# Cosformer attention into a squared-ReLU MLP: loading the first half of w_in in four pieces

## The chip, the cores and the metric

The kernel runs on one core of a Trainium2 chip. The metric is the device time of one execution in microseconds, as the median of several executions; lower is better.

## The reference, cut to what matters

Eight batches of eight heads, 576 positions and a head width of 64 go through a linear attention; its output, 4608 tokens of width 512, goes through an MLP of inner width 2048.

```python
def phi(x, c, s):
    r = np.maximum(x, 0.0)
    return np.concatenate([r * c, r * s], axis=-1)
q_p, k_p = phi(q, cos_w, sin_w), phi(k, cos_w, sin_w)
kv = np.einsum('bhsf,bhsd->bhfd', k_p, v)
z = np.sum(k_p, axis=2)
num = np.einsum('bhsf,bhfd->bhsd', q_p, kv)
den = np.einsum('bhsf,bhf->bhs', q_p, z)[..., None] + 1e-06
x = (num / den).transpose(0, 2, 1, 3).reshape(B * S, H * D)
r = np.maximum(x @ w_in, 0.0)          # w_in: 512 x 2048
return (r * r) @ w_out                 # w_out: 2048 x 512
```

All inputs and the output are float32. The kernel multiplies in bf16: the loads of w_in and w_out, which GpSimd (POOL) issues, convert on the way.

## The kernel before, in words

**Tiling.** A batch's 576 positions are four blocks of 128 (j = 0 to 3) and a tail of 64 (j = 4). Two blocks make a "half" of 256 tokens. For one batch the attention makes features of k and q (lines 404 to 410), sums k against v with a column of ones (kz), copies that sum to SBUF (kvz), transposes the q features, multiplies (num), divides (div) and transposes the result into xT, which has the 512 inputs of the MLP as four row blocks (kb) of 128. A row block holds two heads, so kb 0 and 1 come from the first four heads (group g = 0) and kb 2 and 3 from the last four (g = 1).

**The first MLP product.** `declare_plain` (line 712) makes one *pair*: two blocks of 128 inner columns (hb and hb + 1) for one half of tokens. It is eight matmuls of 256 token columns on TensorE (PE), into one PSUM bank. A ReLU on ScalarE (ACT, line 416) empties the bank into `rt`, and a square on VectorE (DVE, line 419) writes `gT`. Batch 0 has eight pairs for each of its two halves. Only the first two pairs, hb = 0 and hb = 2 of half 0, are made in two steps of 128 tokens (`split`), so that the first can begin before the second block's xT is there. From batch 3 on the products use seven multiplications in place of eight, with sums of w_in's blocks (`w1s`) that DVE makes early. The second product (`declare_rows` for batch 0, then `declare_pair`) reads `gT` and w_out (`w2sb`).

**The start.** `prologue` (line 1069) issues the loads of batch 0 on SyncE's queue (SP): k, k's tail, q for j = 0 and 1, v's tail, v in two groups of heads, q for j = 2 and 3, and at the end q's tail, `qt`, in two DMAs. POOL waits until v's tail has landed (line 1090) and then issues w_in in four quarters of 512 columns (`load_w1`, lines 371 to 376). TensorE runs `fill` matmuls on zeros meanwhile. POOL then issues, in the planner's order, the loads of batch 1, w_out in four quarters, and the loads of batch 2. Later batches are loaded from SP.

**What sets the order.** Each engine works through its own list in order, so an instruction that waits holds up all behind it on its engine. The lists are written by a planner (lines 52 to 230) while the program is built. Each operation is declared with its possible engines, a cost, and what it reads and writes. The planner walks forward in a planned time: each engine takes the operation that can begin first, among equals the one with the earliest due time, and the engine, if there is a choice, is settled that way too. PE operations have a slot in place of a due time. `SHIFTS` (lines 21 to 34) changes the due time or slot of single operations by their number, and fixes the engine of some (`23:9.5:ACT`). Data loaded in the prologue enter the plan as `given`, with a time of arrival (lines 1098 to 1106). PSUM has six banks in the pool "F" for all such products. Key ("w1", n) stands for a quarter n of w_in: a pair hb reads ("w1", hb // 4).

Of the kernel before, what the change touches and what calls it, by code (L numbers as in the profile page):

```python
# [18 lines left out]


SHIFTS = """
23:9.5:ACT 37:-0.5 38:1.0 44:17.5:ACT 46:-1.0 53:-0.5 62:11.5 79:-2.0 85:-2.5 89:3.0 93:11.0
108:5.5 144:9.0 152:-2.0 157:9.5:ACT 191:-5.0 194:-1.0 202:-1.5 203:-3.5:ACT 204:2.0 210:3.0
238:2.5 241:2.5 243:5.0 249:-6.0 257:-4.0 260:-2.0 261:-6.0 270:2.5 271:3.5 287:-5.0 325:-2.0
335:-0.5 340:1.5 348:8.5 354:-7.0 364:-19.0 383:1.0 390:-3.5 392:1.0 417:-4.5 487:-5.0 492:1.5
516:-7.5 517:-5.5 530:39.0 533:25.5 546:9.0 563:5.5 565:12.5 573:-8.5 575:5.0 588:13.0 593:4.5
598:-2.0 611:-4.5 617:-5.5 636:-1.5 670:7.5 677:-2.0 690:1.0 698:0.0:DVE 702:22.5 703:-19.5
704:3.5:ACT 706:-4.0 715:2.0 731:-2.5 748:5.0 781:-4.5 783:-6.0 785:-7.0 787:-2.0 790:-1.0
794:-1.5 797:1.0 799:1.0 807:11.0 813:-5.5 817:-4.0 820:-7.0 822:-5.5 836:-3.5 850:-3.5
859:-34.0 860:-15.0 870:1.0 872:-4.0 884:12.0 890:49.0 893:17.0 906:5.5 907:23.5 911:3.0 917:3.0  # L30
936:-3.0 951:-12.5 957:-1.0 958:-1.5 963:-3.5 985:7.0 990:-4.0 998:3.5 1005:-4.5 1009:5.5
1023:-10.0 1024:-8.5 1030:-10.0 1041:-26.0:ACT 1042:-10.5 1133:-13.0 1143:1.5 1155:4.0 1157:3.0
1176:-4.5 1191:4.5 1209:5.5 1247:2.5 1306:-0.5
"""


# [197 lines left out]
def kernel(  # L234
# [9 lines left out]
    nc = tc.nc  # L244
    P = nc.NUM_PARTITIONS
# [4 lines left out]
    KB = DM // P  # L250
# [7 lines left out]
    HBH, KB2, DM2, TP = HB // 2, KB // 2, DM // 2, 2 * P  # L258
# [104 lines left out]
    def load_tail(src, nm, i, b, eng):  # L363
        tail = mem[nm + "t"][:, i]
        for g in range(2):
            eng.dma_start(  # L366
                out=tail[g * TAIL : (g + 1) * TAIL, :, :],
                in_=src[b, g * HH : (g + 1) * HH, MAIN:S, :].rearrange("h p d -> p h d"),
            )

    def load_w1(i, n):
        f0, f1 = i * DFF // n, (i + 1) * DFF // n
        nc.gpsimd.dma_start(  # L373
            out=w1sb[:, :, f0:f1],
            in_=moe_w_in[:, f0:f1].rearrange("(kb p) f -> p kb f", p=P),
        )
# [60 lines left out]
    T_MM, T_MM128, T_MM65, T_TR = 0.1092, 0.0586, 0.0296, 0.066  # L437
    plan = Planner(POOLS, 4.5, ("gs1", "gs2", "gs3", "gs4"), 1.0, SHIFTS)
    add = plan.add
    PROD1, PROD2 = 4 * T_MM, 8 * T_MM  # L440
# [5 lines left out]
    T1, T2, t = {}, {}, 16.4  # L446
    for b in range(B):
        T1[b], T2[b] = t, t + g1_len[b] + att_len / 2
        t = T2[b] + g2_len[b] + att_len / 2
# [51 lines left out]
    def xT_of(b, half):  # L501
        return cached(xTb, (b, half), "xT")
# [196 lines left out]

    def w1_at(kb, hb):
        return w1sb[:, kb, hb * P : (hb + 1) * P]

    def gkey(hb, half):
        return ("g", hb // 2, half)

    def xT_keys(b, half, cs):
        xT = xT_of(b, half)
        return [(xT, c) + g for c in cs for g in (((0,), (1,)) if (b, half) == (0, 0) else ((),))]  # L710

    def declare_plain(b, hb, half, pos, split=False):

        bk, rt = plan.buf("F"), plan.buf("rt")
        xT = xT_of(b, half)
        for c in range(2) if split else (None,):

            def plain(_, c=c):
                c0, c1 = (0, TP) if c is None else (c * P, (c + 1) * P)
                for i in range(2):  # L720
                    for kb in range(KB):
                        mm(
                            bank(bk)[:, i * TP + c0 : i * TP + c1],
                            w1_at(kb, hb + i),
                            at(xT)[:, kb, c0:c1],
                            i == 0 and kb == 0 and c0 == 0,
                            kb == KB - 1,
                        )

            add(  # L730
                ("PE", 8 * (T_MM128 if split else T_MM)), plain,
                r=xT_keys(b, half, (0, 1) if c is None else (c,)) + [("w1", hb // 4)],
                w=[bk], pos=pos + (c or 0) * PROD2,
            )
        add(
            ("ACT", 0.5), lambda _: relu(at(rt), bank(bk).rearrange("p (i c) -> p i c", i=2)), r=[bk], w=[rt],
        )
        add(
            ("DVE", 0.34),
            lambda _: square(gT[:, hb : hb + 2, half * TP : (half + 1) * TP], at(rt)),  # L740
            r=[rt], w=[gkey(hb, half)],
        )
# [3 lines left out]
    def declare_tails(b, hb, pos):  # L746

        bk, rt = plan.buf("F"), plan.buf("rt")
        xT = xTt_of(b)
        gt = cached(gttb, b // 4, "gTt")  # L750

        def tails(_):
            for i in range(2):
                for kb in range(KB):
                    mm(
                        bank(bk)[:, i * TP : (i + 1) * TP].rearrange("p (m c) -> p m c", m=4),
                        w1_at(kb, hb + i),
                        at(xT)[:, :, kb % 2, kb // 2, :],
                        i == 0 and kb == 0,
                        kb == KB - 1,  # L760
                    )

        add(("PE", PROD2), tails, r=[(xT, m) for m in range(4)] + [("w1", hb // 4)], w=[bk], pos=pos)
        add(("ACT", 0.5), lambda _: relu(at(rt), bank(bk).rearrange("p (i c) -> p i c", i=2)), r=[bk], w=[rt])
        add(
            ("DVE", 0.34),
            lambda _: square(at(gt)[:, hb : hb + 2, :], at(rt)),
            r=[rt], w=[(gt, hb // 2)],
        )
# [8 lines left out]
    def declare_w1_sums():  # L778
        for r in range(4):
            a = lambda i, kk, r=r: w1_cols(i, kk, r)  # L780
            s = lambda n, r=r: w1_sum(n, r)
            key = lambda i: ("w1", (i * HBH + 2 * r) // 4)
            for n, in0, in1, op, reads in (
                (1, a(1, 0), a(1, 1), ALU.add, [key(1)]),
                (2, s(1), a(0, 0), ALU.subtract, [key(0), ("w1s", 1, r)]),
                (4, a(0, 1), s(2), ALU.subtract, [key(0), ("w1s", 2, r)]),
                (3, a(0, 0), a(1, 0), ALU.subtract, [key(0), key(1)]),
            ):
                add(
                    ("DVE", 0.34), lambda _, n=n, x=in0, y=in1, op=op, s=s: sub(s(n), x, y, op),  # L790
                    r=reads, w=[("w1s", n, r)],
                )
# [17 lines left out]
    def declare_seven1(b, r, t):  # L810
# [12 lines left out]
        def product(name, off, acc, w, x, first, reads):  # L823
# [11 lines left out]
            seven.__name__ = name  # L835
            add(("PE", PROD1), seven, r=reads, w=[acc], pos=t + off * PROD1)

        key = lambda i: ("w1", (i * HBH + 2 * r) // 4)
        product("P1", 0, A, lambda: w1_cols(0, 0, r), lambda: X(0, 0), True, [key(0), turn] + xk[0])
        add(("ACT", 0.5), lambda _: nc.scalar.copy(out=bank(Bk), in_=bank(A)), r=[A], w=[Bk])  # L840
        product("P2", 5, A, lambda: w1_cols(0, 1, r), lambda: X(1, 0), False, [key(0)] + xk[0])
# [10 lines left out]
            r=[E, u3], w=[(rows[1], 1)],  # L852
# [4 lines left out]
            r=[E, u2], w=[(rows[0], 1)],  # L857
# [210 lines left out]

    def prologue():
        for src, nm, part in (  # L1070
            (k, "k", 0), (k, "kt", 0), (q, "q", 0), (v, "vt", 0), (v, "v", 0), (v, "v", 1), (q, "q", 1), (q, "qt", 0)
        ):
            if nm[1:]:
                load_tail(src, nm[0], 0, 0, nc.sync)
            elif nm == "k":
                load_main(src, nm, 0, 0, nc.sync)
            elif nm == "q":
                load_main(src, nm, 0, 0, nc.sync, [slice(part * J // 2, (part + 1) * J // 2)])
            else:
                h = slice(part * HH, (part + 1) * HH)  # L1080
                nc.sync.dma_start(
                    out=mem["v"][:, 0, h],
                    in_=v[0, h, 0:MAIN, :].rearrange("h (p j) d -> p h j d", j=J),
                )
        nc.vector.memset(zeros, 0.0)
        for t in ("vx", "vxt"):
            nc.vector.memset(mem[t][:, :, :, D:E1], 1.0)
        constants()
        fill(28)
        nc.gpsimd.tensor_copy(out=w1sb[0:1, 0, 0:1], in_=mem["vt"][0:1, 0, 0, 0:1])  # L1090
        for i in range(4):
            load_w1(i, 4)

    def fill(n):
        for _ in range(n):
# [3 lines left out]
    L = lambda nm: loaded[nm, 0]  # L1099
    for keys, t in (  # L1100
        ([L("k")], 6.25), ([L("kt")], 6.7), ([(L("q"), 0)], 8.2), ([L("vt")], 9.0), ([(L("v"), 0)], 10.75),
        ([(L("v"), 1)], 12.15), ([(L("q"), 1)], 14.2), ([L("qt")], 14.6),
    ):
        given(keys, t, lat=0.0)
    for i in range(4):
        given([("w1", i)], 11.7 + 0.01 * i, size=2.6)

    def declare_first():
        feature = lambda nm, j, c: declare_feature(nm, 0, j, c, BOTH)
# [139 lines left out]
        declare_xT_pe(0, j, t + 4.0, BOTH)  # L1249
    for s in range(8):  # L1250
        for i in range(2):
            declare_plain(0, s % 4 * 4 + 2 * i, s // 4, T1[0] + s * 2 * PROD2 + i * PROD2, s == 0)
    declare_load(1, "q", "POOL", 17.0)
    declare_w2_load(0, 19.0, 10.0)
    declare_load(1, "k", "POOL", 20.0)
# [44 lines left out]
        for i, pair in enumerate(PAIRS[b]):  # L1300
            declare_pair(b, pair, T2[b] + i * 7 * PROD2)

    t0 = {"PE": 8.0, "ACT": 6.3, "DVE": 6.3, "SP": 10.0, "POOL": 12.9, "GIVEN": 0.0}
    with tc.manual_schedule():
        prologue()
        end = None
# [35 lines left out]
```

## Time and profile before

| what | value |
|---|---|
| time, three runs | 277.09 us median (276.61 to 277.94) |
| the profiled execution's own time | 276.82 us |
| its span in the profile | 274.8 us |
| PE busy | 267.9 us (98%) |
| DVE, ACT, POOL busy | 218.9, 194.9, 21.6 us |
| w_in's four DMAs on POOL's queue | issued from 9.12 us, 512 KB each as written |
| first MLP product | 16.48 us |

The span is the profiled program from its first instruction; the 2.0 us between it and the execution's own time lie around it. A line such as L430 is often that of a helper: all matmuls have L430, so groups are told apart by their tiles. "q0" is POOL's DMA queue, "q1" that of SP. A PE row gives the time from the first matmul's start to the last one's end; matmuls follow each other faster than one lasts, so spacings are read from the starts of neighbouring rows. A wait is named by the operation that ended it.

### The profile page before, as it was taken

How to read it: one execution, taken by the hardware profiler on the slowest of the kernel's cores; microseconds unless marked ns; L12 is line 12 of the kernel's file. 1: busy time of each engine (PE TensorE's matmuls, PEld its weight loads, DVE VectorE, ACT ScalarE, POOL GpSimd, SP SyncE). 2: the span in 40 equal slices, each digit the busy share in tenths (PEclk: the TensorE clock that was granted, in tenths of full speed). 3: DMA queues.
4: the chain of work that ended last, by engine and by line, in shares of the span. 5: the costliest groups of instructions: out<-in, count | busy, mean ns of one | idle time of the engine just before them, and what ended most of it. 6: DMA issues, size and time to landing. Idle time of an engine off the chain costs nothing.

```text
span 274.8 us, 7115 instructions
## 1 busy us (share of the span) xinstructions
PE 267.9 (98%) x2845; PEld 227.6 (83%) x2845; DVE 218.9 (80%) x515; ACT 194.9 (71%) x391; POOL 21.6 (8%) x38
## 2 busy tenths in 40 slices
PE   8979999999999999999999999999999999999994
PEld 3668856789988988888888898988988888888884
DVE  1789996997694989699968999799968798279652
ACT  3876982997895598589957994699735954684522
POOL 1453544010000000000000000000000000000000
PEclk9999999999999999999999999999999999999999
DMA  7999999969979998899299955996198301200025
GB/s 217 321 205 290 296 283 365 219 218 225 361 160 186 281 334 156 224 347 221 81 164 308 259 181 102 265 338 217 35 205 170 91 2 44 95 16 2 1 79 153
DMA packets 81840, 53.01 MB, mean 193 GB/s; under 512 B 53584, under 2 KB 77648, under 8 KB 81808
## 3 DMA queue, kind: packets, MB, share of 16 engines
q1 hardware_dynamic: 75136, 40.12, 58.4%
q0 software_dynamic: 6528, 12.32, 17.1%
q8 instruction: 22, 0.36, 0.5%
q10 hardware_dynamic: 144, 0.13, 0.1%
q14 instruction: 10, 0.08, 0.1%
HBM read 36.70 MB, written 9.44 MB: 168 GB/s over the span
## 4 chain that ended last, share of the span: by engine, by line
PE 80%; DMA 8%; DVE 7%; issue 1%; SPq 1%; POOL 1%; ACT 1%; DVEq 0%
PE banks L430 79%; DMA w1sb<-in_moe_w_in_dram 4%; DMA qpT<-qp 2%; DMA vt<-in_v_dram 2%; DVE rs L422 2%; DVE gT L419 2%; DVE gs L427 2%; PE banks L591 1%; DVE x L639 1%; POOL w1sb L373 1%; SPq L366 0%; PE banks L682 0%; DVE qp L408 0%; DVE kp L408 0%; SPq L358 0%
## 5 line engine op out<-in xcount | busy, mean ns | idle before, releaser
L430 PEld LDWEIGHTS <-w1sb 128*128 128x128 bf16 x784 | 73.0, 98 | 10.4 <-DMA w1sb<-in_moe_w_in_dram 1.4
L430 PE MATMUL banks<-xT,w1sb 128*128 128x256 bf16 (+1 forms) x576 | 68.4, 267 | 1.0 <-DMA w1sb<-in_moe_w_in_dram 1.0
L430 PEld LDWEIGHTS <-gs 128*128 128x128 bf16 x512 | 49.0, 98 | 5.9 <-DVE gs L427 0.2
L416 ACT ACTIVATE rt<-banks 128x512 bf16<-128x512 f32 x64 | 37.2, 600 | 14.9 <-PE banks L430 9.3
L430 PEld LDWEIGHTS <-gT 128*128 128x128 bf16 x400 | 38.0, 98 | 9.0
L430 PE MATMUL banks<-w2sb,gT 128*128 128x256 bf16 (+1 forms) x288 | 44.2, 296 | 0.0
L430 PEld LDWEIGHTS <-w1s 128*128 128x128 bf16 x320 | 30.7, 98 | 3.7
L430 PE MATMUL banks<-w2sb,gs 128*128 128x256 bf16 x256 | 33.0, 273 | 0.0
L430 PE MATMUL banks<-w2s,gs 128*128 128x256 bf16 x256 | 32.2, 273 | 0.0
L422 DVE CUSTOM_DVE_ANT_0 rs<-banks,sums 128x512 bf16<-128x512 f32 x40 | 27.0, 684 | 4.5 <-ACT sums L847 3.1
L419 DVE TENSOR_TENSOR gT<-rs 128x1024 bf16<-128x1024 bf16 (+1 forms) x50 | 27.7, 579 | 1.8 <-ACT rs L416 1.0
L416 ACT ACTIVATE rs<-banks 128x512 bf16<-128x512 f32 x40 | 23.6, 604 | 3.1 <-PE banks L430 2.9
L430 PE MATMUL banks<-xs,w1s 128*128 128x256 bf16 x160 | 23.0, 273 | 0.0
L430 PE MATMUL banks<-xT,w1s 128*128 128x256 bf16 x160 | 22.9, 273 | 0.0
L419 DVE TENSOR_TENSOR gT<-rt 128x512 bf16<-128x512 bf16 x48 | 19.2, 418 | 4.5 <-ACT rt L416 4.3
L427 DVE TENSOR_TENSOR ysb<-banks,sums 128x256 f32<-128x256 f32 x32 | 13.4, 418 | 11.2 <-PE banks L430 7.3
L406 ACT ACTIVATE qp<-q,sin_col 128x512 bf16<-128x512 f32 x31 | 22.1, 738 | 0.1
L639 DVE TENSOR_TENSOR x<-banks,den 128x512 bf16<-128x512 f32 x30 | 20.7, 691 | 1.0
L406 ACT ACTIVATE kp<-k,sin_col 128x512 bf16<-128x512 f32 x30 | 21.2, 734 | 0.0
L427 DVE TENSOR_TENSOR gs<-gT 128x1024 bf16<-128x1024 bf16 x28 | 19.2, 686 | 1.1 <-PE banks L430 0.7
L413 ACT CAST vx<-v 128x512 bf16<-128x512 f32 x26 | 16.2, 636 | 0.9 <-DMA v<-in_v_dram 0.9
L637 DVE TENSOR_SCALAR den<-banks 128x8 f32<-128x8 f32 (+1 forms) x38 | 6.0, 159 | 12.5 <-PE banks L430 12.3
(106 smaller groups left out, 364.0 us busy)
## 6 DMA issues: line engine op xcount, KB each, us to landing
out_dram<-ysb SPq DMA_DIRECT2D x13, 512.0 KB, 3.5
k<-in_k_dram SPq DMA_DIRECT2D x6, 1024.0 KB, 6.4
v<-in_v_dram SPq DMA_DIRECT2D x5, 1024.0 KB, 7.9
q<-in_q_dram SPq DMA_DIRECT2D x5, 1024.0 KB, 9.3
w1sb<-in_moe_w_in_dram POOLq DMA_DIRECT2D x4, 512.0 KB, 10.5
q<-in_q_dram POOLq DMA_DIRECT2D x2, 1024.0 KB, 11.2
w2sb<-in_moe_w_out_dram POOLq DMA_DIRECT2D x4, 512.0 KB, 11.6
k<-in_k_dram POOLq DMA_DIRECT2D x2, 1024.0 KB, 11.3
```

What stands on the lines that cost most here:

```text
L373: nc.gpsimd.dma_start(out=w1sb[:, :, f0:f1], in_=moe_w_in[:, f0:f1].rearrange("(kb p) f -> p kb f", p=P),)
L406: nc.scalar.activation(out=dst, in_=src, func=ACTF.Relu, scale=col)
L413: (nc.scalar.copy if eng == "ACT" else nc.vector.tensor_copy)(out=out, in_=in_)
L416: nc.scalar.activation(out=out, in_=in_, func=ACTF.Relu)
L419: nc.vector.tensor_tensor(out=out, in0=in_, in1=in_, op=ALU.mult)
L422: nc.vector._custom_dve(TENSOR_ADD_SAT, out=out, in0=in0, in1=in1, s0=float("inf"), s1=0.0)
L427: nc.vector.tensor_tensor(out=out, in0=in0, in1=in1, op=op)
L430: nc.tensor.matmul(out=out, lhsT=lhsT, rhs=rhs, start=start, stop=stop, skip_group_check=True)
L591: nc.tensor.transpose(t[:, h, :], qp_at(b, j)[:, h, :], ident[:, :])
L637: nc.vector.tensor_single_scalar(out=d, in_=n4[:, :, :, D], scalar=EPS, op=ALU.add)
L639: nc.vector.tensor_tensor(out=x_at(b, j).rearrange("p (b k) (l d) -> p b k l d", b=n, l=2), in0=n4[:, :, :, 0:D].rearrange("p b (k l) d -> ...
```

## The change

The change is confined to how batch 0 starts, and to the planner's inputs. In the program's order view of both kernels PE has eight matmuls fewer, POOL four DMAs more and SP two fewer.

- Quarters 0 and 1 of w_in are loaded as four pieces of 256 columns; quarters 2 and 3 stay whole. The keys become ("w1", 0) to ("w1", 5), through `w1_key`.
- `qt` of batch 0 goes from the end of SP's prologue to POOL's queue, behind the last piece of w_in.
- The first two pairs are made in three steps each: both blocks of tokens with kb 0 and 1 (which need the first four heads only), then kb 2 and 3 for each block of 128 tokens.
- The arrivals in `given`, POOL's first planned time (12.9 to 15.2) and the whole list `SHIFTS` are new. The list applies to the numbers of the operations, which move by two to four. In the order that results, 33 operations have another engine of ACT and DVE: 18 go from ACT to DVE and 15 from DVE to ACT. Matmul groups trade places in all batches.

```diff
 SHIFTS = """
-23:9.5:ACT 37:-0.5 38:1.0 44:17.5:ACT 46:-1.0 53:-0.5 62:11.5 79:-2.0 85:-2.5 89:3.0 93:11.0
...
+45:1.5:ACT 61:2.0 68:-3.0:DVE 89:2.0 98:-2.0 100:5.0 106:6.0 109:6.0 142:5.0 190:-4.0 202:1.5
...
+    def w1_key(hb):
+
+        return ("w1", hb // 2 if hb < 8 else 2 + hb // 4)
+
...
-        for c in range(2) if split else (None,):
-
-            def plain(_, c=c):
-                c0, c1 = (0, TP) if c is None else (c * P, (c + 1) * P)
+        whole = (0, KB, 0, TP, 0.0)
+        parts = [whole]
+        if split and b == 0:
+            parts = [(0, KB2, 0, TP, 0.0), (KB2, KB, 0, P, 4 * PROD1), (KB2, KB, P, TP, 4.5 * PROD1)]
+        elif split:
+            parts = [(0, KB, 0, P, 0.0), (0, KB, P, TP, PROD2)]
+        for k0, k1, c0, c1, later in parts:
+
+            def plain(_, k0=k0, k1=k1, c0=c0, c1=c1):
                 for i in range(2):
-                    for kb in range(KB):
+                    for kb in range(k0, k1):
...
-            (k, "k", 0), (k, "kt", 0), (q, "q", 0), (v, "vt", 0), (v, "v", 0), (v, "v", 1), (q, "q", 1), (q, "qt", 0)
+            (k, "k", 0), (k, "kt", 0), (q, "q", 0), (v, "vt", 0), (v, "v", 0), (v, "v", 1), (q, "q", 1)
...
         for i in range(4):
+            load_w1(i, 8)
+        for i in range(2, 4):
             load_w1(i, 4)
+        load_tail(q, "q", 0, 0, nc.gpsimd)
...
-        ([(L("v"), 1)], 12.15), ([(L("q"), 1)], 14.2), ([L("qt")], 14.6),
+        ([(L("v"), 1)], 12.15), ([(L("q"), 1)], 13.8),
...
-    for i in range(4):
-        given([("w1", i)], 11.7 + 0.01 * i, size=2.6)
+    for i, t in enumerate((14.6, 15.9, 17.3, 18.6, 21.2)):
+        given([("w1", i)], t, lat=0.0)
+    given([("w1", 5)], 14.0, size=7.7)
+    given([L("qt")], 14.1, size=0.45)
...
-            declare_plain(0, s % 4 * 4 + 2 * i, s // 4, T1[0] + s * 2 * PROD2 + i * PROD2, s == 0)
+            declare_plain(0, s % 4 * 4 + 2 * i, s // 4, T1[0] + s * 2 * PROD2 + i * (PROD2 if s else PROD1), s == 0)
...
-    t0 = {"PE": 8.0, "ACT": 6.3, "DVE": 6.3, "SP": 10.0, "POOL": 12.9, "GIVEN": 0.0}
+    t0 = {"PE": 8.0, "ACT": 6.3, "DVE": 6.3, "SP": 10.0, "POOL": 15.2, "GIVEN": 0.0}
```

## The prediction

> **What bounds the kernel now.** I read the busy shares first, then the chain of work that ended last, then the PE timeline of the first 24 us, and last the DMA queues stretch by stretch.
>
> ```profile
> span 274.8 us, 7115 instructions
> PE 267.9 (98%) x2845; PEld 227.6 (83%) x2845; DVE 218.9 (80%) x515; ACT 194.9 (71%) x391; POOL 21.6 (8%) x38
> ```
>
> PE is never idle for long, so what can be won is idle PE time, and the question is where it lies. The chain in order of time shows what PE waited for:
>
> ```profile
> 9.12 1.66 POOL w1sb L373 x2
> 10.78 11.36 DMA w1sb<-in_moe_w_in_dram
> 22.19 1.05 PE banks L430 x8
> ```
>
> The end of the kernel follows from one DMA: the third quarter of w_in, for which PE waits until 22.19. The PE timeline shows the waits one by one (start, length, what, in brackets the idle time before):
>
> ```profile
> 16.48 0.61 PE L430 MATMUL banks<-xT,w1sb 128*128 128x128 bf16 x8
> ...
> 19.64 1.05 PE L430 MATMUL banks<-xT,w1sb 128*128 128x256 bf16 x8 [0.86 <-DMA w1sb<-in_moe_w_in_dram]
> ...
> 22.19 1.05 PE L430 MATMUL banks<-xT,w1sb 128*128 128x256 bf16 x8 [0.16 <-DMA w1sb<-in_moe_w_in_dram]
> ...
> 23.52 8.90 PE L430 MATMUL banks<-xT,w1sb 128*128 128x256 bf16 x80
> ```
>
> The quarters thus arrive at 16.3 (issue 9.12 plus the shortest time to landing of w_in's DMAs, 7.2), 19.6, 22.15 and 24.7 (issue 11.5 plus the longest, 13.2). From 23.52 on PE runs dense; the stretches show about 0.54 us of idle PE between there and the last product (0.34 in 114 to 137, 0.20 in 137 to 150). The DMA view of 13 to 16 us (packets, MB written, share of 16 engines), then a line of that of 16 to 20:
>
> ```profile
> q0 software_dynamic: 542, 0.54, 107.0%
> q1 hardware_dynamic: 256, 0.06, 16.1%
> ```
>
> ```profile
> DMA packets 810, 0.83 MB, mean 207 GB/s; under 512 B 16, under 2 KB 809, under 8 KB 809
> ```
>
> The 256 packets on q1 are one of the two DMAs of q's tail. The engines are full here, so w_in moves at their rate: 0.18 MB per us beside the tail, 0.207 alone.
>
> **What the Trainium skill says.** "DMA: Bandwidth & Descriptors", section "Queues, rings and completion order": each DMA engine takes turns between the queues that have work, packet by packet. The trace agrees: q1's small packets took a turn beside q0's in 13 to 16 us. Its "Specifications" put the shortest transfer at full rate at 512 B. A row of a 256-column piece is exactly 512 B as written; before has only 1 KB rows of w_in, so no row here shows it. "TensorE: Matmul & The Clock Gate", section "Back-to-back issue gap", gives 55.6 ns between matmuls of 128 columns; here eight took 0.44 us to the next row (16.48 to 16.92), 55 ns, and 80 of 256 columns took 8.82 us (23.52 to 32.34), 110 ns.
>
> **The change part by part.**
>
> *q's tail out of the way of w_in.* Two DMAs of 256 packets. The one in 13 to 16 cost q0 (0.207 - 0.18) x 3 = 0.08 MB, 0.39 us at 0.207. The other lies in 12 to 13, where the engines are as full, and costs the same: 0.8 us together. Bounds: 0.4 (only the first counts) and 0.97 (16.1% of 3 us, twice). Taken: 0.8. Issued on POOL behind w_in, it lands about 0.4 to 1 us after w_in's end.
>
> *Four pieces for two quarters.* As many packets per piece as per quarter (512), half as long. Lower bound of the cost: none, if bytes decide; a gain has no reason, since the same bytes go through the same full engines. Next row: q1's 1 KB packets of f32 at 8 to 12 us moved 359 GB/s; w_in is read as f32, 2 x 207 = 414 GB/s. At 359 the first half, 2.1 MB read, takes 5.84 us for 5.07: 0.8 more. Upper bound: a half packet costs a whole one, 2 x 2.53 = 5.1 us more. I take 0.2, since 157 smaller packets are in the 359.
>
> So the first half's pieces land near 15, 16, 17.5 and 19, and the third quarter at 22.15 - 0.8 + 0.2 = 21.55 (21.0 to 22.5 without the packet bound; w_in ends near 24.1).
>
> *When PE asks for it.* In the new order the first product is the depth half of hb = 2, which reads the second piece (near 16.0) and the xT copies of g = 0 (done at 15.40 before). It starts at 16.0, hardly before 16.48. Up to hb = 10, the first of the third quarter, PE then has: 8 half-depth matmuls (0.87), hb = 4 and 6 (1.75), 16 of 128 columns (0.90), two num groups (0.25 each) and two groups of four transposes (0.22 each): 4.46, so it asks at 20.5, with 0.2 more for the copies of xT. It waits until 21.6: one wait of about 1 us in place of 0.86 and 0.16. The halves of depth take nothing off: 8 matmuls of 110 ns and 16 of 55 for 32 of 55, 1.76 us both ways. They only put work where PE had to wait.
>
> *What that is worth.* At that point both kernels have the same work left: hb = 8 to 14 of half 0, all eight pairs of half 1, the transposes of the last x block and those of q's tail. Before starts it at 22.19, after at 21.6. **Gain 0.6 us.** It is no larger because the third quarter, not the first, ends last.
>
> *The wait for q's tail.* ACT has its feature ahead of the ReLU of half 1's first pair, DVE ahead of the square of hb = 8. Both reach it near 23.5 and q's tail lands near 25: ReLUs and squares behind it stand for 1.5 us. PE doesn't notice, because the six F banks let it go on until half 1's hb = 8 wants the bank of half 1's hb = 0 again, six pairs (5.2 us) after 22.9, near 28. The transposes of the tail stand at 29 in the new order. Cost 0; if the tail came after 27, PE would wait for the difference.
>
> *POOL's queue.* Six issues at 0.78 and two at 0.62 end near 15.1; the next, batch 1's q, waits for its buffer until 16.35 as before. Cost 0. q0 stays full, so what follows lands by bytes: batch 1's tail of q is moved behind w_out and makes room for batch 0's. w_out's quarters and batch 1's v (whose casts began at 39.25) come some 0.6 us earlier too, so the lead isn't lost there. SP only loses two issues.
>
> *Priorities.* Work doesn't change; order does. Later waits leave 0.54 us to win. DVE gets longer until batch 5: by counts and durations (0.48 a feature, 0.69 a copy of eight transposes, 0.34 to 0.42 the rest) about 3.2 us are added up to 137 us, 1.6 come off behind it. DVE has room ahead of that: it is busy 1.54 of 4 us in 110 to 114, 6.27 of 10 in 80 to 90. In 114 to 137 it is the tight one (21.90 of 23); only about 0.3 of the 3.2 is added there. I take 0 net, -0.5 to +3.
>
> **The sum.** 276.82 (span 274.8 and 2.0 around it) - 0.6 = 276.2 for a profiled execution. That execution lay 0.27 under the median of the three runs, so the median should be 277.09 - 0.6 = 276.5.
>
> **Rivals.**
> 1. *More is won.* Half packets cost nothing (gain 0.8) and the new order also removes the later 0.54: 275.7. For: bytes set the rate of a full engine. Against: each new order has waits of its own.
> 2. *The gain is eaten, or the change does nothing at the front.* The third quarter comes no sooner (packets at 359 GB/s cost the 0.8 that the tail gives), or a later wait takes the lead: 277.1. For: the wait is moved, not removed.
> 3. *Slower: DVE late in 114 to 137.* The place is the squares and sums for batch 3's products, with DVE at 21.90 of 23 us. If the 3.2 us added up to there aren't absorbed, PE waits for them: 277.09 - 0.6 + 3.2 = 279.7. It decides once more than 0.6 us arrive unabsorbed, and is plain from 2.0 us. For: in that stretch the chain that ended last runs over DVE. Against: 2.46 us free just ahead.
> 4. *Half packets cost whole ones.* The third quarter at 26.6, which PE awaits: 277.09 + 4.5 = 281.6.
>
> **How the numbers follow.** Forecast (gain 0.3 to 1.2) 0.35, rival 1 0.22, rival 2 0.20, rival 3 0.17, rival 4 0.06. A measurement of this kernel tells 0.5%, 1.4 us, from no change: below 275.7 is faster, above 278.5 slower. Most of rival 1 ends near that line, so faster gets 0.20; slower is rivals 3 and 4, 0.23; the same 0.57. The range 275.2 to 279.0 leaves out rival 4, the worst of rival 3 and the best of rival 1. The likeliest case alone: 275.9 to 276.8.
>
> **What would show it.** Right: a wait for w_in of about 1 us ahead of hb = 10, ending near 21.6, and dense PE from there; w_in's end near 24.1; POOL's issue of batch 1's q still at 16.4; ACT and DVE idle for q's tail near 24 with no PE wait by 28. Wrong: pieces that take 1.5 us or more each; PE waits of over 0.6 us in all behind 30 us, above all for DVE in 114 to 137; or a first product well before 16.

## The result and the profile after

The change made the kernel slower: 280.36 us (median of four runs, 280.12 to 280.86) against 277.26 for the kernel before (four runs, the three of above among them). The ratio is 1.0123, 95% interval 1.0088 to 1.0158. The profiled execution took 280.86 us, with a span of 279.1. Its span is 4.3 us longer than that of before, more than the 3.1 us between the medians, since it was the slowest of the four. Line numbers have moved: L428 is L430 of before (all matmuls), L404 is L406 (features), L411 is L413 (casts and copies), and the copies out of PSUM have numbers higher by six (L964 for L958).

The head of the page of the changed kernel, then its line of busy time:

```profile
span 279.1 us, 7107 instructions
...
PE 269.5 (97%) x2837; PEld 227.3 (81%) x2837; DVE 220.5 (79%) x518; ACT 193.5 (69%) x388; POOL 25.2 (9%) x42
```

PE's work is the same (its matmuls at the spacings given below add up to the same time within 0.02 us), so what was added is idle time. The front first; these are PE's rows between 16 and 24 us, to be read as those of before:

```profile
16.69 0.61 PE L428 MATMUL banks<-xT,w1sb 128*128 128x256 bf16 x4
...
20.05 1.26 PE L428 MATMUL banks<-xT,w1sb 128*128 128x128 bf16 x12
21.90 1.05 PE L428 MATMUL banks<-xT,w1sb 128*128 128x256 bf16 x8 [0.59 <-DMA w1sb<-in_moe_w_in_dram]
```

There is one wait for w_in that the view names, as the change meant it, and it ends at 21.90 where that of before ended at 22.19. Of these 0.29 us, 0.17 are not the change's: POOL issued w_in at 8.95, in before at 9.12, since v's tail landed sooner in that execution (9.31 in `after_again`).

```profile
8.95 4.65 POOL L371 DMA_DIRECT2D w1sb<-in_moe_w_in_dram  x6 [0.31 <-POOL w1sb L1096]
```

From w_in's issue to the end of the wait, two traces of the kernel before took 13.07 and 13.41 us, two of the changed one 12.95 and 13.14. The DMA view of 13 to 16 us says in part why the front wins so little (queue, packets, MB written, share):

```profile
q0 software_dynamic: 1080, 0.54, 136.4%
q1 hardware_dynamic: 41, 0.02, 2.3%
```

q's tail is gone from q1, yet q0 moves no more than it did beside the tail: the same 0.54 MB in 3 us, now in twice as many packets.

The loss lies behind the front. Parts of the chain of waits, in order of time (start, length, what), now look like this:

```profile
12.08 9.78 DMA w1sb<-in_moe_w_in_dram
...
63.58 6.38 DMA k<-in_k_dram
70.03 0.72 ACT kp L404
71.03 1.26 ACT kp L404 x2
...
96.95 7.55 DMA kt<-in_k_dram
104.53 0.91 ACT kpt L404 x2
...
115.65 8.75 DMA v<-in_v_dram
124.44 0.50 issue
124.94 0.59 ACT rs L414
```

Before, the chain ran over PE alone for long stretches. Now it goes from a load of a later batch to ACT and then to PE. DMA has 24% of it (8% before), PE 54% (80%). The share by itself is no sign of a loss: DMA has 20% of the chain in `old_order_tail_moved` below, which is not slower than before. What matters is where PE waits. ACT's waits for DMAs, in the view of waits (in all, times, longest):

```profile
ACT kp L404 <- DMA k<-in_k_dram: 4.7, 3, 3.1
...
ACT vx L411 <- DMA v<-in_v_dram: 2.5, 4, 1.0
ACT ysb L966 <- DMA out_dram<-ysb: 1.7, 2, 0.9
ACT qp L404 <- DMA q<-in_q_dram: 1.5, 2, 0.9
ACT kpt L404 <- DMA kt<-in_k_dram: 1.4, 2, 1.0
```

In before only the first two stood there, with 3.7 and 0.9 us. PE's own waits are small and many. Counted from the starts (the distance between two neighbouring groups, less what the first one's matmuls take at 110 ns for 256 columns), PE lost 1.05 us behind 24 us in before, in three places of over 0.1 us, and 5.10 us in fifteen such places now. Four of them, in PE's timeline (the bracket shows a little less than the starts do):

```profile
71.08 1.03 PE L428 MATMUL banks<-w2s,gs 128*128 128x256 bf16 x8 [0.36 <-ACT banks L964]
...
106.05 1.03 PE L428 MATMUL banks<-w2s,gT 128*128 128x256 bf16 x8 [0.33 <-ACT sums L973]
...
126.55 0.60 PE L428 MATMUL banks<-xs,w1s 128*128 128x256 bf16 x4 [0.27 <-ACT banks L846]
137.06 1.03 PE L428 MATMUL banks<-w2sb,gs 128*128 128x256 bf16 x8 [0.21 <-ACT sums L968]
```

The reason at 71 us is plain from ACT's own timeline in the changed kernel:

```profile
70.03 0.72 ACT L404 ACTIVATE kp<-k,sin_col 128x512 bf16<-128x512 f32 x1 [1.30 <-DMA k<-in_k_dram]
70.66 0.36 ACT L964 COPY banks<-banks 128x256 f32<-128x256 f32 x1
```

and from the same stretch in the kernel before:

```profile
68.39 0.36 ACT L958 COPY banks<-banks 128x256 f32<-128x256 f32 x1 [0.52 <-PE banks L430]
69.36 0.59 ACT L413 CAST kvz<-banks 128x520 bf16<-128x520 f32 x1 [0.61 <-PE banks L430]
70.33 0.37 ACT L962 COPY sums<-banks 128x256 f32<-128x256 f32 x1 [0.38 <-PE banks L430]
70.60 0.72 ACT L406 ACTIVATE kp<-k,cos_col 128x512 bf16<-128x512 f32 x1
```

The load of batch 3's k lands close to 70 us in both (69.79 in before, 69.95 now). In before the first copy out of PSUM stands ahead of the features that need this load. The new order has a feature ahead of the copy, and the copy, whose operand was there at 68.9, waits behind it.

### The profile page after: what moved, and what is told of

Its sections match the earlier page's. It is cut to its first block, busy times and chain, and to the rows that moved or that the text cites. A ratio compares the mean times of both kernels' runs of the same rounds, so it can differ in the third digit from the quotient of the medians.

```text
span 279.1 us, 7107 instructions
## 1 busy us (share of the span) xinstructions
PE 269.5 (97%) x2837; PEld 227.3 (81%) x2837; DVE 220.5 (79%) x518; ACT 193.5 (69%) x388; POOL 25.2 (9%) x42
## 4 chain that ended last, share of the span: by engine, by line
PE 54%; DMA 24%; DVE 6%; ACT 6%; SPq 4%; issue 3%; POOL 2%; POOLq 0%; DVEq 0%; ACTq 0%
PE banks L428 54%; DMA v<-in_v_dram 8%; DMA k<-in_k_dram 7%; DMA w1sb<-in_moe_w_in_dram 4%; DMA kt<-in_k_dram 3%; DMA vt<-in_v_dram 2%; SPq L364 2%; SPq L356 1%; DVE gT L417 1%; POOL w1sb L371 1%; ACT qp L404 1%; DMA out_dram<-ysb 1%; DVE rs L420 1%; ACT kp L404 1%; ACT vx L411 1%
## 5 line engine op out<-in xcount | busy, mean ns | idle before, releaser
L428 PEld LDWEIGHTS <-w1sb 128*128 128x128 bf16 x776 | 72.6, 98 | 9.3 <-DMA w1sb<-in_moe_w_in_dram 0.9
L428 PE MATMUL banks<-xT,w1sb 128*128 128x256 bf16 (+1 forms) x568 | 68.5, 268 | 0.6 <-DMA w1sb<-in_moe_w_in_dram 0.6
L428 PEld LDWEIGHTS <-gs 128*128 128x128 bf16 x512 | 49.6, 98 | 7.9 <-issue 1.7
L428 PEld LDWEIGHTS <-gT 128*128 128x128 bf16 x400 | 37.7, 98 | 9.4 <-issue 0.5
L428 PE MATMUL banks<-w2sb,gT 128*128 128x256 bf16 (+1 forms) x288 | 44.8, 296 | 0.0
L428 PEld LDWEIGHTS <-w1s 128*128 128x128 bf16 x320 | 30.6, 98 | 4.9 <-issue 0.9
L428 PE MATMUL banks<-w2sb,gs 128*128 128x256 bf16 x256 | 32.8, 272 | 0.8 <-DVE ysb L425 0.4
L428 PE MATMUL banks<-w2s,gs 128*128 128x256 bf16 x256 | 32.2, 273 | 0.4 <-ACT banks L964 0.4
L428 PE MATMUL banks<-xs,w1s 128*128 128x256 bf16 x160 | 23.2, 273 | 0.5 <-ACT banks L846 0.5
L404 ACT ACTIVATE qp<-q,sin_col 128x512 bf16<-128x512 f32 x32 | 22.1, 720 | 1.5 <-DMA q<-in_q_dram 1.5
L428 PE MATMUL banks<-xT,w1s 128*128 128x256 bf16 x160 | 22.5, 273 | 0.1
L404 ACT ACTIVATE kp<-k,sin_col 128x512 bf16<-128x512 f32 x29 | 20.5, 726 | 1.6 <-DMA k<-in_k_dram 1.6
L411 ACT CAST vx<-v 128x512 bf16<-128x512 f32 x26 | 16.2, 630 | 2.5 <-DMA v<-in_v_dram 2.5
L428 PE MATMUL banks<-xTt,w1sb 128*128 128x256 bf16 x128 | 15.9, 273 | 0.0
```

The source lines that it names most:

```text
L404: nc.scalar.activation(out=dst, in_=src, func=ACTF.Relu, scale=col)
L411: (nc.scalar.copy if eng == "ACT" else nc.vector.tensor_copy)(out=out, in_=in_)
L428: nc.tensor.matmul(out=out, lhsT=lhsT, rhs=rhs, start=start, stop=stop, skip_group_check=True)
```

## The experiments

**Theory A**: the loss lies in the order that the new SHIFTS and arrivals give. **Theory B**: it lies in the loads of the front, whose shifted landings run on through the kernel. To separate them, most kernels below take a written list in place of the planner's walk. It holds the operations with their engines and the places of the buffers, recorded from one planner's run, so that one operation can be moved while all others stay:

```diff
-        for op in plan.plan(t0):
...
+        for b, i in zip(ALLB, PLACES.split()):
+            b.i = int(i)
...
+                op = plan.ops[int(t.rstrip("ADSOG"))]
+                op.eng = names.get(t[-1], "PE")
+                op.fn(op.eng)
```

All ratios are to the kernel before on the same chip, with 95% intervals. How far to trust them was measured too, with the kernel before run as if it were another kernel (`before_again`):

> The kernel before itself, to have its trace from the same chip: 1.000 within 0.2 per cent; TensorE's waits behind 30 us at 1 to 2 us in all.

It gave **0.9962 (0.9946 to 0.9979)**, for 1.000 within 0.2% expected. Nothing differs, so a ratio here can be off by 0.4%, twice what its interval says. For some kernels the plain quotient of the medians is also smaller than the ratio, by up to 0.4% (1.0068 for 1.0104 in `after_again`). Steps below that size need a second witness, from the trace or from a repeat. A trace shows one execution, which lay up to 1.7 us from the median of its kernel.

### Order or loads

Only the pieces, in before's order:

```diff
         for i in range(4):
+            load_w1(i, 8)
+        for i in range(2, 4):
             load_w1(i, 4)
```

> The kernel before, order of all engines untouched; only the first half of w_in comes in four pieces. Theory A (the loss of the change lies in the order that the new priorities give): 277.3 to 277.9, that is 0 to 0.6 over before: the pieces make the third quarter about 0.5 us later, and PE's wait at hb=10 ends so much later; no wait over 0.3 us comes up behind 50 us that before doesn't have. Theory B (the loss comes from the loads of the front, whose lateness runs on through the kernel): 279 or more.

The whole front in before's order. Batch 0's query tail gets a place in `ysb` (`qt0`), and its operations are moved in the list:

```diff
+    qt0 = mem["ysb"][:, 0, 0, 0 : HH * D].rearrange("p (h d) -> p h d", d=D)
...
+        tail = qt0 if (nm, b) == ("q", 0) else mem[nm + "t"][:, i]
```

> The whole front of the changed kernel (four pieces, batch 0's query tail behind w_in on POOL's queue, first products in halves of depth) with the order of the kernel before for everything else; only the two features, the transpose and the copy of the query tail are moved behind its landing, and its tile gets a place of its own so that batch 1's tail need not wait for it. Theory A: 276.6 to 277.2, so 0 to 0.6 under before, with PE's waits behind 30 us at about 1.1 us as in before. Theory B: 279 to 280.5, with about 5 us of waits.

This one had a fault of its own: the tail's transpose held a PSUM bank that a later product needed, and PE lost 1.42 us at 29 us. Its successor has another bank (2 for 4) and the copy earlier:

> As old_order_new_front (the changed kernel's whole front, before's order for everything else), with its own fault taken out: there the transpose of the query tail held the bank that the product four steps later needed, and TensorE waited 1.4 us for it at 29 us; here it has a bank that is free for longer and its copy comes earlier in DVE's list. Theory A (the loss lies in the new order): 0.2 to 1.2 us under before on the same chip, waits of TensorE behind 30 us at 1 to 2 us. Theory B (the loss comes from the front's loads): 1.5 us or more over before.

The counterpart, the new order on the old loads, is the changed kernel with before's prologue:

```diff
-            (k, "k", 0), ..., (q, "q", 1)
+            (k, "k", 0), ..., (q, "q", 1), (q, "qt", 0)
...
-            load_w1(i, 8)
-        for i in range(2, 4):
             load_w1(i, 4)
-        load_tail(q, "q", 0, 0, nc.gpsimd)
```

> The changed kernel's order on every engine and its halves of depth, but with before's loads: w_in in four quarters, batch 0's query tail ahead of it on SP's queue. Theory A: 280 to 281, the waits of ACT and PE behind 50 us stay where the changed kernel has them (53.8, 71, 73, 106, 126.5, 137, 212 us), about 4 us in all over before. Theory B: 277 to 278.

And the changed kernel itself:

> The changed kernel itself once more, to stand beside the others on one chip: 1.009 to 1.016 of before by both theories, with TensorE's waits behind 50 us again at 71 to 76, 106, 126 and 137 us if they belong to the order (theory A), at other places if they are chance.

| loads | order | ratio to before |
|---|---|---|
| old, but in pieces | old | 0.9977 (0.9958 to 0.9996) |
| new front, with the fault | old | 1.0084 (1.0054 to 1.0114) |
| new front | old | **1.0007** (0.9986 to 1.0028) |
| old | new | **1.0102** (1.0065 to 1.0139) |
| new front | new (`after_again`) | **1.0104** (1.0058 to 1.0149) |

The new front alone costs nothing and wins nothing that can be measured; the new order costs about as much as the whole change, with either loads. Theory B falls. The two rows that decide it are `old_order_new_front_b` and `after_again`, with the same front on the same chip: 1.0007 and 1.0104, or 278.61 and 280.72 us in the medians. The pieces alone, expected to cost up to 0.6 us, show no cost (0.9977), though PE's wait for the third quarter ended at 23.32 in that trace.

Two things were not as expected. PE's waits behind 30 us in `old_order_new_front_b` were to be 1 to 2 us; its trace has 3.4, but that execution took 280.26 us, 1.65 over its median. And part of the 1.0102 of `new_order_old_loads` is a front of its own: this order asks for hb = 4 sooner than whole quarters bring it, and PE waits longer there than before did:

```profile
20.46 1.49 PE L428 MATMUL banks<-xT,w1sb 128*128 128x256 bf16 x16 [0.92 <-DMA w1sb<-in_moe_w_in_dram]
```

At 68 us its PE is 0.93 us behind that of the changed kernel at the same product. The waits behind 100 us then come where they were expected (105.8, 126.7, 137.5 and 212 us), but those at 53.8 and 71 to 76 us do not. ACT has the same list there, feature ahead of copy, but k had landed at 68.06, and nothing waits:

```profile
69.49 0.71 ACT L404 ACTIVATE kp<-k,sin_col 128x512 bf16<-128x512 f32 x1
70.10 0.37 ACT L964 COPY banks<-banks 128x256 f32<-128x256 f32 x1
```

So that place costs only when its load is late. In `after_again`, with k at 69.21, PE lost 0.73 us at 72 to 76; the waits near 125, 136 and 211 us came again, that at 106 did not.

The tail's move without the pieces was tried as well, since the pieces might cost what the move wins:

> Before's order, w_in in four whole quarters as before; only batch 0's query tail is loaded behind w_in (its features, transpose and copy moved as in old_order_new_front_b). If the tail ahead of w_in cost time, the quarters land about 0.4 to 0.9 us earlier and the end comes 0.3 to 0.9 us under before; if the pieces are what gains, it equals before within 0.3.

It gave 0.9984 (0.9964 to 1.0005). PE's wait for the third quarter ended at 22.28, 22.19 in before:

```profile
22.28 1.05 PE L432 MATMUL banks<-xT,w1sb 128*128 128x256 bf16 x8 [0.16 <-DMA w1sb<-in_moe_w_in_dram]
```

From w_in's issue (9.26) that is 13.02 us, for 13.07 and 13.41 in the two traces of before. Neither half of the front is worth anything that shows.

### One place put in, six and nine taken out

At 68 us the kernel before gets the changed kernel's fault (ACT's list):

```diff
-bank copy L958, kvz, copy L962, feature k, copy L958, feature k, copy L960, feature k, feature k
+feature k, bank copy L958, feature k, feature k, kvz, copy L962, copy L958, feature k, copy L960
```

> The kernel before with one thing of the new order put in: at 68 us on ACT three features of batch 3's k (which wait for their load until about 69.9 us) stand ahead of the two bank copies and the kvz copy that TensorE waits for. Theory A: TensorE waits 1 to 2 us between 70 and 74 us and nearly all of it stays to the end: 1 to 2 us over before. If such waits are made good later (slack in the rest), under 0.4 us over before.

1.0056 (1.0025 to 1.0088); the medians, 279.56 and 278.82 us, are 0.74 us apart. Its PE rows:

```profile
71.04 1.03 PE L430 MATMUL banks<-w2s,gs 128*128 128x256 bf16 x8 [1.92 <-ACT banks L958]
...
126.62 0.60 PE L430 MATMUL banks<-xs,w1sb 128*128 128x256 bf16 x4 [1.63 <-ACT sums L847]
```

The wait comes where the changed kernel has it, it is not made good later in this trace (2.9 us more span than before's), and the wait at 124 us (0.34 in before) has grown. The time alone is near the uncertainty of 0.4%; with the trace as second witness, features ahead of copies do cost where their load is late. The other way round, in the changed kernel, the operations that wait for a load were put behind the copies (ACT at 69 to 76, 104, 124 and 135 us; DVE at 52 and 156):

```diff
 ACT, 69 to 71 us, then 104 us
-feature k, copy L964, feature k, feature k, copy L964, kvz
+copy L964, feature k, copy L964, kvz, feature k
...
-feature kt, feature kt, cast vt, copy L973
+copy L973, feature kt, feature kt, cast vt
```

> The changed kernel, loads untouched; only in six places of ACT's and DVE's lists operations that wait for a load or a store (or need nothing yet) are put behind the copies from PSUM that TensorE waits for: near 53, 71 to 76, 106, 126, 136 to 138 and 157 us. Theory A: the waits there, 3.6 of 5.1 us, mostly go: 277 to 278.2. Theory B: the lateness comes up at the next place, 279.5 or more.

1.0080 (1.0057 to 1.0102). The waits at 71 to 76, 126 and 137 us are gone. But behind 100 us others stand in their place:

```profile
106.99 1.03 PE L428 MATMUL banks<-w2sb,gT 128*128 128x256 bf16 x8 [0.58 <-ACT banks L964]
138.62 1.03 PE L428 MATMUL banks<-w2s,gT 128*128 128x256 bf16 x8 [0.50 <-ACT sums L973]
```

Three more places were mended there:

> As new_order_mended, with three more places of ACT's list set right where that kernel's trace showed a bank copy behind operations on loaded data: near 106, 136 to 139 and 180 to 183 us. If each place is a cost of its own (theory A): 0.6 to 1.2 us under new_order_mended, 1.003 to 1.006 of before. If a mended place only hands the wait on: again 1.007 to 1.010.

1.0096 (1.0076 to 1.0117); the wait came up at the next operation, now for the cast of v:

```profile
108.21 0.40 PE L428 MATMUL banks<-vx,kp 128*128 128x65 bf16 x8 [0.52 <-ACT vx L411]
```

Theory A holds for the order as a whole, but not in its first form, in which each misplaced copy is a cost by itself. Behind 100 us ACT seems to be late, whatever stands first in its list.

### Which half

At 88 us both orders have done exactly the same operations and hold the same buffers, so the lists can be joined there.

> The changed kernel (loads, halves of depth and all) with its own order on every engine up to 88 us and before's order from there on; at that point both orders have done exactly the same operations and hold the same buffers, so nothing else is touched. If the loss of the order (about 1.0 per cent, 2.8 us) is made in the first part (waits at 53 and at 71 to 76 us): 1.005 to 1.008 of before. If it is made behind 88 us: 0.998 to 1.002.

> The other half: the changed kernel's front loads with before's order up to 88 us (as old_order_new_front_b) and the changed kernel's order from there on. If the loss is made in the first part: 1.000 to 1.003 of before. If it is made behind 88 us (waits at 106 to 110, 126, 137, 212 us): 1.005 to 1.010. The two halves together should give the 1.010 to 1.012 of the whole order, if they add.

> old_until_88 once more, as the base of kt_first on this chip: 1.005 to 1.010 of before by both theories, TensorE's waits again near 106, 110 and 127 us.

New up to 88 us: 1.0027 (1.0007 to 1.0046). New from 88 us: 1.0073 (1.0053 to 1.0094), again 1.0065 (1.0034 to 1.0095). The halves add up to the whole within the uncertainty, and the larger loss is made behind 88 us. Whether the first half costs anything is not shown: 1.0027 is under the 0.4%, and in the trace of `new_until_88`, where k landed at 67.47, PE has no wait of over 0.1 us between 24 and 88 us.

### Mixed lists

Three kernels were to tell PE's order behind 88 us from the lists of the other engines:

> As old_until_88, but behind 88 us only TensorE's order (and the buffers that go with it) is the changed kernel's; ACT's, DVE's and SP's lists are before's as nearly as that allows (136 of 765 pairs out of turn are left). If the lists of ACT, DVE and SP cost (theory A as first put): 1.000 to 1.003 of before. If TensorE's own order costs (it asks for products in a sequence whose operands or banks come later): 1.005 to 1.009.

> The mirror: behind 88 us TensorE's order is before's, and ACT's, DVE's and SP's lists are the changed kernel's as nearly as that allows. If the lists cost: 1.004 to 1.008 of before. If TensorE's order costs: 1.000 to 1.003.

> As old_until_88, with SP's list alone behind 88 us as before's: the small tail of k directly behind k and ahead of v and q, the DMA transposes of x earlier in the queue. If the loads that land late (the tail of k at 104 us, ACT waiting for it) carry the loss: 1.001 to 1.004 of before, and ACT no longer waits at 104 us. If SP's list is not what costs: 1.006 to 1.009 as old_until_88.

They gave 1.2087 (1.2039 to 1.2135), 1.1220 (1.1172 to 1.1268) and 1.0364 (1.0317 to 1.0412). All are far outside what any theory said, and they say nothing on the 0.7%. PE's order and the lists belong to one plan; where one is taken from another plan, an engine's list can wait for things that the others make much later. In the traces single waits of PE reach 8.9 us at 194 us (`pe_order_only`), 4.4 at 178 (`lists_only_new`) and 4.0 at 191 (`sp_list_old`). The misses show only how far a list can be from fitting.

### The first link of the chain

SP's queue tells what makes ACT late. In `old_until_88_again` (start, length, what; the length of an issue is the time SP was held by it):

```profile
89.45 0.58 SPq L358 DMA_DIRECT2D k<-in_k_dram  x1
90.08 0.58 SPq L358 DMA_DIRECT2D v<-in_v_dram  x1
90.70 1.16 SPq L358 DMA_DIRECT2D q<-in_q_dram  x1
91.91 4.47 SPq L366 DMA_DIRECT2D kt<-in_k_dram  x2
96.42 2.50 SPq L366 DMA_DIRECT2D vt<-in_v_dram  x2
...
102.97 2.64 SPq L667 DMA_TRANSPOSE xT<-x  x2
```

Batch 4's tail of k (kt, two pieces of 64 KB) is issued behind three loads of 1 MB. Its two issues hold SP for 4.47 us, and ACT has the features of this tail ahead of a copy for PE:

```profile
103.23 0.51 ACT L406 ACTIVATE kpt<-kt,cos_col 128x256 bf16<-128x256 f32 x1 [0.51 <-DMA kt<-in_k_dram]
```

So the query features, their transposes and the loads of batch 5 that follow these in SP's queue are late, and ACT waits again, until 123.7 us, for batch 5's v. The changed kernel has the same list (kt at 93.54, held 4.46 us; the transposes of x at 104.18). The kernel before has kt directly behind k:

```profile
88.83 0.58 SPq L358 DMA_DIRECT2D k<-in_k_dram  x1
89.45 1.29 SPq L366 DMA_DIRECT2D kt<-in_k_dram  x2
90.78 0.60 SPq L358 DMA_DIRECT2D v<-in_v_dram  x1
...
98.84 4.78 SPq L667 DMA_TRANSPOSE xT<-x  x2
```

The order in the queue sets when the tail lands. In the eight traces with kt behind v and q (both of the changed kernel among them) its second piece landed at 102.2 to 104.5 us, within 0.5 us of q. In the twelve with kt directly behind k (both of before among them) it landed at 95.3 to 98.2.

One swap on one queue tests the chain:

```diff
 SP, 89 us
-k, v, q, kt, vt, qt
+k, kt, v, q, vt, qt
```

> old_until_88 with one swap in SP's queue: batch 4's tail of k is issued directly behind its k, ahead of v and q. If the chain from that load carries the loss: the tail lands before 100 us, ACT doesn't wait for it, TensorE's waits at 106, 110 and 127 us (2.2 us in old_until_88) shrink to under 0.8 us, and the time is 1.5 to 2.2 us under old_until_88_again. If lateness only moves: within 0.6 us of it.

1.0021 (1.0002 to 1.0041), 279.05 us against 280.22 for `old_until_88_again` on the same chip: 1.2 us from the swap. That size alone is near the 1.06 us by which the two medians of one kernel differed. The trace is the second witness. SP's queue in `kt_first`, then ACT's feature of the tail:

```profile
89.53 1.28 SPq L366 DMA_DIRECT2D kt<-in_k_dram  x2
...
99.09 4.81 SPq L667 DMA_TRANSPOSE xT<-x  x2
```

```profile
102.01 0.56 ACT L406 ACTIVATE kpt<-kt,cos_col 128x256 bf16<-128x256 f32 x1
```

No wait of ACT for kt is left. PE's waits of 0.42 and 0.53 us at 105 and 110 us (from the starts) are gone, that of 0.93 near 126 is 0.61: together 1.27 us, for 1.2 in the time. The transposes of batch 4's queries are issued at 105.4 (108.1), batch 5's v at 113.05 (114.90). Of these leads 0.54 us stood already at 89 us, ahead of the swap, where k was issued at 88.91 (89.45). The expectation of under 0.8 us in these places held; the expected 1.5 to 2.2 us in the time did not quite. Last, the same swap in the changed kernel itself, with the mended places at 52 (DVE) and 69 to 76 us (ACT):

> The changed kernel with the same swap in SP's queue, and with only two mended places of new_order_mended (DVE near 53 us, ACT at 69 to 76 us). If both chains are what costs: 1.001 to 1.005 of before. If lateness only moves: 1.008 to 1.012.

**1.0038 (1.0020 to 1.0057)**, 1.0104 and 1.0123 for the changed kernel without them. By these ratios the swap and the mended places together take away some two thirds of the loss. The share is rough, as the ratios come from different sets of runs and each can be off by 0.4%, and what each takes away alone in this kernel is not shown. No version beat the kernel before by more than `before_again` did.

## Why the prediction was wrong

It said 276.5 us, 275.2 to 279.0; it was 280.36. By its own steps:

- **The bound at the front** was read rightly: the third quarter of w_in ends last there, the view names one wait in place of two, PE is dense behind it for a while, q's tail is waited for by ACT (2.8 us against 1.5 predicted) at no cost to PE, and batch 1's q is issued by POOL at 16.09 (16.4 predicted).
- **q's tail out of the way, 0.8 us**, is not borne out. `old_order_tail_moved` is this step alone, and from w_in's issue to the end of the wait it won 0.05 to 0.39 us (13.02 for 13.07 and 13.41).
- **Four pieces for two quarters** was mis-sized: 0.2 us taken, about 0.5 by this estimate: 0.54 MB in 13 to 16 us, for 0.62 at 0.207 MB per us, and 0.79 in 16 to 20, for 0.81 in before, make 0.1 MB or 0.5 us. The prediction also had 0.8 by the rate of q1's 1 KB packets, and took less. The Trainium skill ("DMA: Bandwidth & Descriptors", "Specifications") puts the shortest transfer at full rate at 512 B. Rows of 512 B as written moved 0.36 MB in 14 to 16 us here, rows of 1 KB 0.41 in the same stretch of `old_order_tail_moved`; in 16.5 to 17.5 us it was 0.19, for 0.20 in before. At first the rate was thus not full, and the measurement decides.
- **The two together**: with 0.5 the sum gives the third quarter at 22.15 - 0.8 + 0.5 = 21.85, and the wait ended at 21.90. That is partly luck, since the 0.8 did not show alone and w_in was issued 0.17 us sooner.
- **When PE asks for it**: the first product stood at 16.69, not 16.0. What ended last was the second piece of w_in, which landed at 16.64, for 16.0 predicted (17.09 and 17.14 in `after_again`); the copies of xT, though later than in before, were done at 16.34. That cost nothing, as the third quarter ended last.
- **What that is worth**: 0.6 predicted, 0.29 in the trace with 0.17 of it from the earlier issue, and with before's order nothing that shows (1.0007). The step took the same work left for the same end. It is true for PE's work and not for PE's time.
- **Priorities: "0 net, -0.5 to +3"** is the step that failed. With the same front on the same chip, before's order gave 1.0007 and the new one 1.0104: the term was +2.7 us (2.1 by the medians), near the end of its own range, where the sum had 0. The prediction priced the new order by counting what each engine does in each stretch, and found DVE tight in 114 to 137. So it had the slower rival there, for DVE. The time went elsewhere: to ACT's list, where features that wait for loads stand ahead of copies that PE waits for, and to SP's, where a small load went behind three large ones. Neither shows in a count of busy time. Both show in the order of the two programs: `kt` moves from second to fourth place in SP's list, and the copy L964 from before to behind a feature of k. The prediction used that order for the first 30 us and for DVE's counts, and said of SP only that it loses two issues.
- **Rival 3** (279.7) was nearest in size, at the wrong engine and place: DVE ended 1.67 of the 5.10 us (0.55 at 53.8, 0.24 at 157.1, 0.19 at 163.4, 0.58 and 0.11 at 211.9 and 234.7), and none of it in 114 to 137. The sign that was named for "wrong", PE waits over 0.6 us in all behind 30 us, showed itself with 5.10. It was set too low: counted from the starts, the kernel before has 1.05 itself, where the prediction, from the brackets, had 0.54.
- **Rival 4** did not come. Its sum counts the 0.2 us twice: 22.15 - 0.8 + 5.06 is 26.4, not 26.6.

What stays open: 1.0038 is left with both places mended, against an uncertainty of 0.4% by `before_again`. Waits in several traces of the new order (in `kt_first_in_after`, from the starts, 0.61 us at 209.9, where a store of the output holds `ysb`, and 0.44, 0.20 and 0.24 at 134.8, 136.3 and 154.9) fit it, and weren't tried one by one. The chain from the tail of k is shown by its landing times and by PE's waits; its size in time, 1.2 us, is near the uncertainty. What the place at 71 us costs alone in the changed kernel wasn't measured.

## What to carry to other kernels

When an order changes, compare the lists engine by engine over the whole kernel, and look for two things: an operation on freshly loaded data ahead of a copy out of PSUM, and a small load moved behind large ones in its queue. Busy shares show neither. Both cost only where the load is late when its turn comes, so they are places to test. A mended place that hands its wait on suggests that the engine is late and not ill sorted: follow its operands back to the queue that issued them.

## What the runs showed that was not expected

- Two sets of runs of one kernel on one chip differed by 0.38%, with an interval of 0.17% either way.
- Each load here gives 16 landing signals, and the last one counts: in the profiled run of `old_order_pieces` twelve of those of the third quarter came by 21.56 us and the last at 23.27, and PE waited until 23.32. In before fifteen came by 21.38 and the last at 22.14. Such a lag, which differs from run to run, is larger than the 0.6 us that the front was to win.
- An issue of a 64 KB piece on SP took 0.61 to 0.63 us with one large load just ahead of it (before) and up to 3.38 us behind three (`old_until_88_again`).
